# A turned weight block copied in halves, weight casts and x loads moved in the opening, and six units' stores cut in two

## The chip, the core and the metric

The kernel runs on one core of a Trainium2 chip. The metric is the device time of one execution in microseconds (us). The time before is 408.87 us, the median of three runs (406.65 to 410.15).

## The reference

A dynamic convolution over seven taps, whose weights are a softmax per head, feeds a small maxout network:

```python
w = softmax(weight_gen, axis=-1)          # (8, 4160, 8 heads, 7 taps)
x_pad = 6 zero rows ahead of x            # x: (8, 4160, 192)
y[b, s, h, :] = sum_k w[b, s, h, k] * x_pad[b, s + k, h, :]   # 24 features a head
h1, h2 = y @ w1, y @ w2                   # (192, 1024) each
out = maximum(h1, h2) @ w_out             # (1024, 192), float32
```

The setup stretches x to 33280 rows of 192 float32, and the output has the same shape.

## The kernel before

**Tiling.** The 33280 rows are laid over 128 partitions, 260 positions ("columns") each. The columns come in batches: batches 0 to 14 have 16 columns, then one of 12 and one of 8. A batch is cut into units: of 4 columns in batches 0 and 1 (units 0 to 7), of 8 columns afterwards (units 8 to 33), and four more at the end (8, 4, 4, 4). A unit of n columns has n tiles of hidden work; each tile makes 1024 float32 per partition in PSUM, which one relu turns into bf16.

**Arithmetic.** max(h1, h2) is computed as h1 + relu(h2 - h1). So TensorE multiplies the transposed y by wd = w2 - w1 (line 336), ScalarE takes the relu out of PSUM (line 346, "rd_t"), TensorE multiplies that by w_out (line 375), and the linear part y @ (w1 @ w_out) is added by six matmuls with the product w10 (line 387). ScalarE copies the results out (line 431, evac), and SP stores them (line 445).

**Weights.** TensorE contracts 64 rows at a time in pairs, so the 192 rows of wd are kept in six blocks of 512 columns: wd blocks 0, 1 and 2 are differences that VectorE writes (diff, "d.0", "d.1", "d.2", line 593), and blocks 3, 4 and 5 are blocks 0, 1 and 2 with their halves of partitions swapped. TensorE makes the swap (turn, "t.0" to "t.2", line 601), and ScalarE copies it out of PSUM (turn_out, "T", line 607). t.0 and t.2 stand side by side in one PSUM tile, and T.0 copies both at once, into blocks 3 and 5; T.1 copies block 4. The table WD says which blocks a tile reads: those of the first 512 hidden features (tiles 0 and 1 of a 4-column unit, "h.0", "h.1") read blocks 0, 2, 3 and 5, those of the second (h.2, h.3) read blocks 1, 2, 4 and 5. w1 is also cast to bf16 on ScalarE in three parts (cast_w1, "c.0" to "c.2", line 611), is transposed on TensorE ("v", line 628), copied out ("V", line 633), and multiplied by w_out ("p", line 647) to give w10 ("C", lines 654 and 656).

**y.** Softmax weights come from ScalarE and VectorE: exponent ("X", line 153), sum ("n", line 168), log ("l", line 172), subtraction ("s", line 177), exponent again into bf16 pairs ("W", line 191). VectorE multiplies x by them ("m", line 211). In batches 0 and 1 TensorE sums the seven taps and transposes in one go ("y", line 281) and ScalarE copies the result out ("e", line 293). From batch 2 on VectorE adds the taps (lines 227, 233, 236), and a transposing transfer on SP's queue (line 245) brings y into the layout that TensorE reads; a one-element copy on GpSimd ("gate", line 253) waits for its landing, and the next loads of x and weight_gen are issued behind it.

**Order.** The schedule is by hand: each engine runs its instructions in the order in which they are recorded. The opening (batches 0 and 1 up to tile 15) is a string of steps, OPENING; each step is one of the letters above with its arguments. "k.n" are n matmuls on constant data. Loads are "lg" (weight_gen of a batch; batches 0 and 1 on SP's queue, later ones on GpSimd's), "xf" (first x, SP), "lw" and "lt" (the weights, in halves, SP; the arguments are the half and 0 for w1, 1 for w2), "lx" (x, GpSimd's queue, cast to bf16 on the way), "lo" (w_out, GpSimd). "@step" behind a load makes it wait for that step. "xa" and "xv" cast the first x on ScalarE and VectorE. After the opening, a loop over groups of tiles (two or three tiles each, line 780) issues hidden work, results of earlier tiles, and through extra() the VectorE work two units ahead.

**Stores.** evac puts the store of a unit's results on SP's queue when the last columns are copied. Stores of the middle units are held back and issued just behind the next transposing transfer.

Of the kernel before, what the change touches and what calls it, by code (L numbers as in the profile page):

```python
# [23 lines left out]
def kernel(  # L24
# [29 lines left out]
    def dcol(c):  # L54

        return (c + ROT) % CPP
# [207 lines left out]
    def half(j):  # L264
        return slice(64 * j, 64 * j + 64)
# [95 lines left out]

    def op_out(c):

        tile_, at = op_at[c // 2]
        return tile_[:, at + c % 2 * 512:at + c % 2 * 512 + D]

    def out_hidden(c, f, r):

        u, i, j = column(c)
        t0 = TILES.index((u, 0))  # L370
        if UNITS[u][2] == 8:
            (rd, k), at = rd_at[t0 + f], j * 512 + i * P
        else:
            (rd, k), at = rd_at[t0 + f // 2], j * 512 + f % 2 * 256 + i * P
        return nc.tensor.matmul(  # L375
            op_out(c), lhsT=rd[half(r), k * 1024 + at:k * 1024 + at + P],
            rhs=wo[half(r), f * D:(f + 1) * D], start=False, stop=(r != j and f == FCH - 1),
            skip_group_check=True,
        )

# [25 lines left out]
    def relay(last):  # L406

        go = nc.scalar.nop()
        for mm in last:
            tc.add_manual_dep(go.ins, mm.ins.name, SYNC, reason="bank of the other half")  # L410
        return go

    def evac(p, n):

        tile_, at = op_at[p]
        o = o_t[0]
        if p == NT // 2 - 1:

            nc.scalar.copy(out=_sub(o_last, 0, [[D, 2], [1, D]]),
                           in_=_sub(tile_, at, [[512, 2], [1, D]]))  # L420
            for j, eng in enumerate((nc.scalar, nc.sync)):
                eng.dma_start(
                    out=bass.AP(tensor=out.tensor, offset=dcol(place(p)[0] + 2 * j) * D, ap=[[CPP * D, P], [1, D]]),
                    in_=o_last[:, j * D:(j + 1) * D],
                )
            return
        runs = [[q for q in range(p, p + n) if column(2 * q)[0] == u]
                for u in range(column(2 * p)[0], column(2 * (p + n - 1))[0] + 1)]
        for qs in runs:
            c, h = place(qs[0])  # L430
            copied = nc.scalar.copy(out=_sub(o, c % 24 * D, [[D, len(qs)], [h * D, 2], [1, D]]),  # L431
                           in_=_sub(tile_, at + (qs[0] - p) * D, [[D, len(qs)], [512, 2], [1, D]]))
        stores = []
        for q in range(p, p + n):
            u, i, _ = column(2 * q)
            if u == NU - 2 and UNITS[u][2] == 8 and i % 2:
                stores.append((nc.sync, place(q)[0] - 1, [4 * D, 2], [1, 2 * D]))
            elif u < NU - 1 and i == UNITS[u][2] // 2 - 1:
                stores.append((nc.sync, place(q)[0] - i, [1, 2 * (i + 1) * D]))
            if u == NU - 1:  # L440
                stores.append((nc.sync, place(q)[0], [2 * D, 2], [1, D]))
        for eng, c, *ap in stores:

            def issue(eng=eng, c=c, ap=ap, o=o):
                eng.dma_start(
                    out=bass.AP(tensor=out.tensor, offset=dcol(c) * D, ap=[[CPP * D, P], *ap]),
                    in_=_sub(o, c % 24 * D, ap),
                )

            if 3 <= u < NU - 3:  # L450
                held.append(issue)
            else:
                while u > 3 and held:
                    held.pop(0)()
                issue()
        return copied
# [33 lines left out]
    def hidden(g, now=(), between=lambda: None, beside=lambda: None, ahead=lambda: None,  # L490
               before=lambda: None, after=lambda: None):


        t0, n = GROUPS[g]
        rd = room(g)
        for t in range(t0, t0 + n - 1):
            hid_tile(t)
        if now:
            out_room(now, "a" if n == 1 and "a" in ps else None)
            last = out_first(now)  # L500
        for t in range(t0, t0 + n - 1):
            relu(rd, t, 1)
        if now:
            go = relay(last)
        hid_tile(t0 + n - 1)
        before()
        if len(now) > 2:
            beside()
        relu(rd, t0 + n - 1, 1)
        ahead()  # L510
        if now:
            out_second(now, go)
            evac(now[0] // 2, len(now) // 2)
        between()
        after()
        if len(now) <= 2:
            beside()
# [31 lines left out]
    w1 = stage.tile([P, F + HF], BF16, name="w1")  # L549
    w1t = stage.tile([P, FCH * D], BF16, name="w1t")  # L550
# [31 lines left out]
    def block(i):  # L582

        return wd[:, i * HF:(i + 1) * HF]

    def features(i, wi):

        return (ws["T", wi] if i == 2 else ws["E", wi])[:, i % 2 * HF:(i % 2 + 1) * HF]
# [4 lines left out]
        return nc.vector.tensor_tensor(out=block(i), in0=a, in1=b, op=ALU.subtract)  # L593

    turned = {}

    def turn(i):

# [4 lines left out]

    def turn_out(i, v=0):

        n = 2 - i
        return (nc.vector.tensor_copy if v else nc.scalar.copy)(out=_sub(wd, (3 + i) * HF, [[2 * HF, n], [1, HF]]), in_=_sub(turned[i], 0, [[512, n], [1, HF]]))  # L607

    def cast_w1(i):

        return nc.scalar.copy(out=w1[:, i * HF:(i + 1) * HF], in_=features(i, 0))

    def w1_transposed(_):

# [16 lines left out]
    def w1_copy(h):  # L631

        return nc.scalar.copy(out=w1t[:, 4 * h * D:4 * (h + 1) * D], in_=turned["v"][:, h * 1024:h * 1024 + 4 * D])  # L633

    def few(n):

# [13 lines left out]
    def w10_copy(i):  # L650

        pw = turned["w"]
        if i == 0:
            return nc.scalar.copy(out=_sub(w10, 0, [[D, 2], [1, D]]), in_=_sub(pw, 0, [[512, 2], [1, D]]))
        to, frm, at = ((64, 0, 0), (0, 64, 512))[i - 1]
        return nc.scalar.copy(out=w10[to:to + 64, 2 * D:3 * D], in_=pw[frm:frm + 64, at:at + D])

    warm = ps["h"].tile([P, 1024], FP32, name="warm", tag="hd")

# [31 lines left out]
    def results_buffer(_):  # L691
# [28 lines left out]
    """  # L720

    make_identity(nc, ident_f)
# [91 lines left out]
```

## Time and profile before

One execution was profiled. It took 407.24 us, of which 405.4 us are the span from the first to the last instruction; the difference, 1.84 us, lies outside the span.

| what | value |
|---|---|
| runs | 406.65, 408.87, 410.15 us |
| profiled execution | 407.24 us |
| its span | 405.4 us |
| granted TensorE clock | 0.999 of full speed |
| VectorE busy | 369.3 us (91%) |
| ScalarE busy | 361.1 us (89%) |
| GpSimd busy | 69.7 us (17%) |
| HBM traffic | 36.55 MB read, 25.56 MB written |

In the profile's lines, PE is TensorE's matmuls, PEld its weight loads, DVE is VectorE, ACT ScalarE, POOL GpSimd, SP SyncE; "q" behind an engine is its DMA-issuing sequencer. A line such as "L346 ACT ACTIVATE rd_t<-hdp x2" names the kernel's line, the engine, the operation, output and input, and the number of instructions that are merged.

Landings of the opening's transfers, from the semaphores in the trace (us from the span's start):

| step | queue | issued | landed |
|---|---|---|---|
| lg.0 | SP | 0.74 | 4.11 |
| xf, columns -6 to -1 | SP | 1.19 | 5.56 |
| xf, columns 0 to 3 | SP | 1.66 | 7.15 |
| w1, w2 parts (8 transfers, 1.5 MB) | SP | 2.12 to 7.16 | 7.64, 8.22, 8.76, 9.92, 10.46, 11.69, 11.93, 13.20 |
| lg.1 | SP | 7.66 | 15.20 |
| lx.0.4.4 | POOL | 5.96 | 12.73 |
| lx.0.12.4 | POOL | 7.98 | 15.33 |
| lx.0.8.4 | POOL | 12.07 | 16.95 |
| lo | POOL | 12.59 | 19.81 |
| lg.3 | POOL | 13.49 | 20.91 |
| lx.1.0.8 | POOL | 17.15 | 23.41 |

### The profile page before, as it was taken

What the parts mean: (1) busy time and instruction counts of PE and PEld (TensorE: products, weight loads), DVE (VectorE), ACT (ScalarE), POOL (GpSimd) and SP (SyncE); (2) the same over time, 40 slices, a digit from 0 to 9 for tenths busy, and PEclk for the clock granted to TensorE, in tenths of its full rate; (3) what the DMA queues carried; (4) which work ended last, traced back from release to release, by engine and by line L of the source; (5) the groups of instructions that cost most, each with busy time, mean ns of one, the idle gap of its engine ahead of it and who ended that gap; (6) DMA issues with size and microseconds to landing.
All of it is one profiled execution on the core that took longest, in us unless ns stands there. A gap on an engine that the chain in (4) does not pass through costs nothing.

```text
span 405.4 us, 16319 instructions
## 1 busy us (share of the span) xinstructions
PE 396.0 (98%) x7503; PEld 321.1 (79%) x7503; DVE 369.3 (91%) x211; ACT 361.1 (89%) x465; POOL 69.7 (17%) x96
## 2 busy tenths in 40 slices
PE   6999999999999999999999999999999999999996
PEld 2688999777777877777777778777777877787995
DVE  6999999999999999999999999999999999998200
ACT  5999899999999989999899999989999899888872
POOL 2211020212112211122220122121112121210100
PEclk9999999999999999999999999999999999999999
DMA  8955569765877656874776667778457847557304
GB/s 262 247 120 106 155 113 173 188 163 136 164 131 207 175 97 113 251 191 80 213 190 106 146 189 189 91 232 189 78 133 217 170 79 210 136 99 197 100 40 157
DMA packets 60019, 63.16 MB, mean 156 GB/s; under 512 B 47545, under 2 KB 48569, under 8 KB 59952
## 3 DMA queue, kind: packets, MB, share of 16 engines
q1 hardware_dynamic: 51952, 40.15, 37.7%
q0 software_dynamic: 7856, 21.89, 27.4%
q8 instruction: 58, 0.95, 0.9%
q10 hardware_dynamic: 144, 0.10, 0.1%
q14 instruction: 9, 0.07, 0.0%
HBM read 36.55 MB, written 25.56 MB: 153 GB/s over the span
## 4 chain that ended last, share of the span: by engine, by line
PE 94%; DMA 3%; ACT 2%; issue 0%; SPq 0%
PE op_ps L375 42%; PE hdc L336 13%; PE hdb L336 13%; PE hda L336 13%; PE op_ps L387 8%; PE yps L281 2%; PE hdp L336 2%; DMA ws0E<-in_moe_w_dram 1%; DMA xs<-in_x_dram 1%; ACT rd_t L346 1%; PE pw L647 0%; ACT wd L607 0%; ACT e_t L153 0%; ACT w1t L633 0%; ACT yt L293 0%
## 5 line engine op out<-in xcount | busy, mean ns | idle before, releaser
L375 PE MATMUL op_ps<-wo,rd_t 64*128 64x192 bf16 x4160 | 210.6, 243 | 0.6 <-issue 0.6
L375 PEld LDWEIGHTS <-rd_t 64*128 64x128 bf16 x4160 | 180.7, 94 | 15.6 <-issue 0.8
L211 DVE TENSOR_TENSOR m_t<-xb,en_t 128x10752 bf16<-128x10752 bf16 (+2 forms) x39 | 187.5, 4817 | 2.0 <-ACT en_t L191 1.9
L336 PEld LDWEIGHTS <-wd 64*128 64x128 bf16 x1824 | 96.3, 94 | 39.2 <-issue 1.9
L346 ACT ACTIVATE rd_t<-hdc 128x1024 bf16<-128x1024 f32 x82 | 84.0, 1025 | 18.1 <-PE hdc L336 16.5
L253 POOL CAST gate<-yt 128x1 f32<-128x1 bf16 x30 | 37.3, 1243 | 272.3 <-DMA yt<-y_t 272.3
L346 ACT ACTIVATE rd_t<-hdb 128x1024 bf16<-128x1024 f32 x81 | 83.7, 1033 | 0.0
L346 ACT ACTIVATE rd_t<-hda 128x1024 bf16<-128x1024 f32 x81 | 83.4, 1030 | 0.0
L227 DVE TENSOR_TENSOR m_t<-m_t 128x4608 bf16<-128x4608 bf16 (+1 forms) x30 | 72.9, 2431 | 0.1
L336 PE MATMUL hdc<-yt,wd 64*128 64x512 bf16 (+1 forms) x552 | 67.9, 353 | 0.0
L431 ACT COPY o_t<-op_ps 128x384 f32<-128x384 f32 (+1 forms) x99 | 56.0, 577 | 12.6 <-PE op_ps L375 12.6
L336 PE MATMUL hda<-yt,wd 64*128 64x512 bf16 (+1 forms) x540 | 67.0, 355 | 0.0
L336 PE MATMUL hdb<-yt,wd 64*128 64x512 bf16 (+1 forms) x540 | 67.0, 355 | 0.0
L387 PE MATMUL op_ps<-w,yt 64*128 64x192 bf16 x780 | 55.4, 243 | 0.0
L387 PEld LDWEIGHTS <-yt 64*128 64x128 bf16 x780 | 38.8, 94 | 14.6 <-issue 0.3
L233 DVE TENSOR_TENSOR m_t<-m_t 128x3072 bf16<-128x3072 bf16 (+1 forms) x30 | 50.1, 1671 | 0.1
L191 ACT ACTIVATE en_t<-wg_t 128x896 bf16<-128x896 f32 (+3 forms) x48 | 35.4, 769 | 2.3 <-PE op_ps L375 2.0
L236 DVE TENSOR_TENSOR y_t<-m_t 128x1536 bf16<-128x1536 bf16 (+1 forms) x30 | 27.4, 915 | 0.6
L168 DVE TENSOR_REDUCE sum_t<-e_t 128x64 f32<-128x448 f32 (+3 forms) x31 | 19.6, 635 | 3.2 <-ACT e_t L153 3.1
L125 POOL DMA_DIRECT2D xb<-in_x_dram x34 | 18.2, 535 | 24.0 <-ACT en_t L191 12.3
L177 DVE TENSOR_TENSOR wg_t<-wg_t,sum_t 128x280 f32<-128x280 f32 (+6 forms) x46 | 22.0, 480 | 0.0
L153 ACT ACTIVATE e_t<-wg_t 128x896 f32<-128x896 f32 (+2 forms) x18 | 15.8, 884 | 2.1 <-DMA wg_t<-in_weight_gen_dram 2.1
(39 smaller groups left out, 111.3 us busy)
## 6 DMA issues: line engine op xcount, KB each, us to landing
out_dram<-o_t SPq DMA_DIRECT2D x27, 768.0 KB, 4.8
xb<-in_x_dram POOLq DMA_DIRECT2D x30, 384.0 KB, 5.3
wg_t<-in_weight_gen_dram POOLq DMA_DIRECT2D x13, 448.0 KB, 6.0
out_dram<-o_t SPq DMA_DIRECT2D x10, 384.0 KB, 3.3
xb<-xb POOLq DMA_DIRECT2D x7, 288.0 KB, 5.1
wg_t<-in_weight_gen_dram SPq DMA_DIRECT2D x2, 448.0 KB, 5.5
xb<-in_x_dram POOLq DMA_DIRECT2D x4, 192.0 KB, 6.1
xs<-in_x_dram SPq DMA_DIRECT2D x1, 576.0 KB, 4.4
```

The costliest lines, as they stand in the source:

```text
L177: nc.vector.tensor_tensor(out=w_t, in0=w_t, in1=_sub(s_ts[b], hs.start, [[1, hs.stop - hs.start], [0, K]]), op=ALU.subtract)
L191: act = nc.scalar.activation(out=_sub(en_ts[b], (o * WGC + ((i or 0) * J + j) * N * K) * 2, [[2 * N, K], [2, N], [1, 2]]), in_=_sub(wg_ts[ ...
L211: return nc.vector.tensor_tensor(out=m_out, in0=x_in, in1=_sub(en_ts[b], at * H * 2, [[2, K * n * H], [0, G // 2], [1, 2]]), op=ALU.mult,)
L227: nc.vector.tensor_tensor(out=taps(0, 1, 3), in0=taps(0, 1, 3), in1=taps(3, 1, 3), op=ALU.add)
L233: nc.vector.tensor_tensor(out=taps(0, 2, 2), in0=taps(0, 2, 2), in1=taps(1, 5, 2), op=ALU.add)
L236: nc.vector.tensor_tensor(out=_sub(y_ts[b], o * D, [[64, 2], [P, 3 * w // 2], [1, 64]]), in0=taps(0, 1, 1), in1=taps(2, 1, 1), op=ALU.add,)
L253: nc.gpsimd.tensor_copy(out=gate, in_=yt[:, 0:1])
L336: nc.tensor.matmul(hid_out(t, f, j), lhsT=wd_at(j, s, f // 4, f % 4 * P, P), rhs=_sub(yt_ts[u][half(j), :], (s + j) % 3 * P, [[3 * P, w // ...
L346: relu_of[t0] = nc.scalar.activation(out=rd[:, k * 1024:(k + n) * 1024], in_=hd[:, at:at + n * 1024], func=AF.Relu)
L375: return nc.tensor.matmul(op_out(c), lhsT=rd[half(r), k * 1024 + at:k * 1024 + at + P], rhs=wo[half(r), f * D:(f + 1) * D], start=False, s ...
L387: nc.tensor.matmul(op_out(c + j), lhsT=yt_ts[u][half(j), (3 * i + (s + j) % 3) * P:(3 * i + (s + j) % 3 + 1) * P], rhs=w10[half(j), s * D: ...
L431: copied = nc.scalar.copy(out=_sub(o, c % 24 * D, [[D, len(qs)], [h * D, 2], [1, D]]), in_=_sub(tile_, at + (qs[0] - p) * D, [[D, len(qs)] ...
```

## The change

- turn_out learns two more steps: T.3 copies only block 3 and T.4 only block 5, 512 columns each. The opening uses T.3, T.4 and T.1 in place of T.0 and T.1.
- The opening's order is new. On the engines this means the following. SP's loads: the same twelve sizes in the same places, with the third parts of the weights and the second halves of w1 and w2 in other places (the second half of w1 is now ninth instead of eleventh, that of w2 eleventh instead of ninth). VectorE: the cast xv stands between the two subtractions s.0.0 and s.0.1; nothing else moves. ScalarE: xa moves ahead of l.0.1 and W.0.0.0, W.0.12 ahead of c.0 and W.0.8 behind it, c.2 ahead of e.0.0, c.1 ahead of e.0.1; then T.3, T.4, X.1, r.0, T.1, r.1; V.1 comes ahead of V.0; some of the later steps of batches 1 to 3 change places. TensorE: 25 constant matmuls instead of 21 at the start and 3 instead of 11 among the turns; h.0 and h.1 ahead of t.1. GpSimd's queue: lx.0.12.4 waits for W.0.12 instead of xa; lx.0.8.4, lo and lx.1.0.8 no longer wait for a step and follow it directly; lg.2 and lg.3 come behind them.
- Stores of units 19 to 24 (PARTED) are issued as two transfers of 384 KB instead of one of 768 KB.
- out_hidden can take all 128 rows at once, and cast_w1, w1_copy and w10_copy can run on another engine; no call uses that.

```diff
-    def out_hidden(c, f, r):
+    def out_hidden(c, f, r=None):
...
+        rows = slice(0, P) if r is None else half(r)
         return nc.tensor.matmul(
-            op_out(c), lhsT=rd[half(r), k * 1024 + at:k * 1024 + at + P],
-            rhs=wo[half(r), f * D:(f + 1) * D], start=False, stop=(r != j and f == FCH - 1),
+            op_out(c), lhsT=rd[rows, k * 1024 + at:k * 1024 + at + P],
+            rhs=wo[rows, f * D:(f + 1) * D], start=False, stop=(r != j and f == FCH - 1),
...
+    PARTED = range(19, 25)
...
             elif u < NU - 1 and i == UNITS[u][2] // 2 - 1:
-                stores.append((nc.sync, place(q)[0] - i, [1, 2 * (i + 1) * D]))
+                w = i + 1
+                for k in range(0, 2 * w, w if u in PARTED else 2 * w):
+                    stores.append((nc.sync, place(q)[0] - i + k, [1, (w if u in PARTED else 2 * w) * D]))
...
     def turn_out(i, v=0):
 
+        to = (nc.vector.tensor_copy if v else nc.scalar.copy)
+        if i > 2:
+            k = i - 3
+            return to(out=block(3 + 2 * k), in_=turned[0][:, 512 * k:512 * k + HF])
         n = 2 - i
-        return (nc.vector.tensor_copy if v else nc.scalar.copy)(out=_sub(wd, (3 + i) * HF, [[2 * HF, n], [1, HF]]), in_=_sub(turned[i], 0, [[512, n], [1, HF]]))
...
+        return to(out=_sub(wd, (3 + i) * HF, [[2 * HF, n], [1, HF]]), in_=_sub(turned[i], 0, [[512, n], [1, HF]]))
...
     OPENING = """
-        lg.0 xf.-6.6 xf.0.4 lt.1.1 lt.0.0 lw.0.1 lw.0.0 lt.1.0 k.1 lw.1.1 lt.0.1 lw.1.0 lg.1 X.0.0.2 X.0.1.2
-        n.0.0.2 n.0.1.2 l.0.0.2 l.0.1.2 s.0.0.2 k.1 W.0.0.0 s.0.1.2 xa.-6.4 W.0.0.1 W.0.8 xv.-2.6 k.19
-        lx.0.4.4@l.0.0.2 lx.0.12.4@xa.-6.4 m.0.0.0 c.0 W.0.12 m.0.0.1 W.0.4 y.0.0 k.3 y.0.1 e.0.0 c.2 d.0 d.2
-        e.0.1 t.0 k.2 c.1 t.2 k.4 T.0 d.1 t.1 k.2 T.1 m.0.4 lx.0.8.4@W.0.4 lo.0@e.0.0 lg.3@e.0.1 h.0 X.1 r.0
-        h.1 r.1 lx.1.0.8@m.0.4 v.0 n.1 V.0 l.1 h.2 y.1 r.2 e.1 m.0.8 s.1 lg.2@r.2 m.0.12 h.3 r.3 h.4 h.5 V.1
-        r.4 W.1.0 W.1.4 m.1.0 y.2 r.5 e.2 h.6 lx.1.8.8@W.1.0 m.1.4 p.0 C.2 h.7 y.3 C.1 lh.2 C.0 r.6 W.1.8 r.7
-        X.2 n.2 A.3 m.1.8 e.3 B.3 h.8 D.3 r.8 Z.0 E.3 A.4 B.4 lx.2.0.8.0@r.8 h.9 l.2 X.3 W.1.12 y.4 e.4 r.9
-        s.2 D.4 h.10 E.4 W.2.0 n.3 r.10 lg.4@r.10 A.5 y.5 h.11 e.5 l.3 m.1.12 B.5 r.11 D.5 h.12 E.5 A.6 B.6
-        h.13 D.6 r.12 y.6 E.6 W.2.8 lx.2.8.8@W.2.8 r.13 A.7 e.6 h.14 h.15 B.7 r.14 r.15 D.7 y.7 E.7 e.7
+        lg.0 xf.-6.6 xf.0.4 lt.1.0 lt.0.0 k.2 lw.0.1 k.19 lw.0.0 lt.1.1 lw.1.0 lt.0.1 X.0.0.2 k.1 n.0.0.2
+        X.0.1.2 lw.1.1 k.1 k.2 n.0.1.2 l.0.0.2 s.0.0.2 xa.-6.4 l.0.1.2 W.0.0.0 lx.0.4.4@l.0.0.2 lg.1 xv.-2.6
+        W.0.0.1 s.0.1.2 W.0.12 c.0 lx.0.12.4@W.0.12 W.0.8 m.0.0.0 m.0.0.1 W.0.4 y.0.0 y.0.1 c.2 e.0.0 c.1
+        e.0.1 d.0 d.2 t.0 k.3 t.2 T.3 d.1 T.4 h.0 h.1 t.1 X.1 r.0 lx.0.8.4 T.1 lo.0 r.1 m.0.4 n.1 v.0 h.2
+        lx.1.0.8 V.1 y.1 r.2 l.1 h.3 e.1 m.0.8 lg.2@l.1 s.1 V.0 m.0.12 r.3 h.4 W.1.0 m.1.0 y.2 h.5 r.4
+        lg.3@m.0.4 p.0 e.2 r.5 h.6 lx.1.8.8 y.3 W.1.8 h.7 lh.2 C.1 C.0 C.2 A.3 W.1.4 X.2 r.6 e.3 B.3 m.1.4
+        h.8 D.3 y.4 r.7 r.8 Z.0 E.3 n.2 X.3 l.2 m.1.8 A.4 e.4 W.1.12 lx.2.0.8.0@r.7 B.4 h.9 D.4 h.10 r.9 E.4
+        s.2 r.10 lg.4@r.9 y.5 W.2.0 A.5 h.11 B.5 h.12 e.5 D.5 n.3 r.11 r.12 A.6 m.1.12 E.5 h.13 B.6 D.6 y.6
+        r.13 E.6 h.14 e.6 l.3 lx.2.8.8@r.13 h.15 r.14 A.7 W.2.8 B.7 y.7 D.7 r.15 e.7 E.7
```

More of the change, by code (lines that the diff above doesn't have):

```diff
@@ L502, in hidden @@
             relu(rd, t, 1)
-        if now:
-            go = relay(last)
+        go = relay(last) if now else None
         hid_tile(t0 + n - 1)
@@ L595 @@
     turned = {}
+    ENG = (nc.scalar.copy, nc.vector.tensor_copy, nc.gpsimd.tensor_copy)
     def turn(i):
@@ L604, in turn_out, with cast_w1 @@
     def turn_out(i, v=0):
+        to = (nc.vector.tensor_copy if v else nc.scalar.copy)
+        if i > 2:
+            k = i - 3
+            return to(out=block(3 + 2 * k), in_=turned[0][:, 512 * k:512 * k + HF])
         n = 2 - i
-        return (nc.vector.tensor_copy if v else nc.scalar.copy)(out=_sub(wd, (3 + i) * HF, [[2 * HF, n], [1, HF]]), in_=_sub(turned[i], 0, [[512, n], [1, HF]]))
-    def cast_w1(i):
-        return nc.scalar.copy(out=w1[:, i * HF:(i + 1) * HF], in_=features(i, 0))
+        return to(out=_sub(wd, (3 + i) * HF, [[2 * HF, n], [1, HF]]), in_=_sub(turned[i], 0, [[512, n], [1, HF]]))
+    def cast_w1(i, eng=0):
+        if eng == 3:
+            return nc.gpsimd.dma_start(out=w1[:, i * HF:(i + 1) * HF], in_=features(i, 0))
+        return ENG[eng](out=w1[:, i * HF:(i + 1) * HF], in_=features(i, 0))
     def w1_transposed(_):
@@ L629, in w1_products, with w1_copy @@
                                  is_transpose=True, skip_group_check=True)
-    def w1_copy(h):
-        return nc.scalar.copy(out=w1t[:, 4 * h * D:4 * (h + 1) * D], in_=turned["v"][:, h * 1024:h * 1024 + 4 * D])
+    def w1_copy(h, eng=0):
+        return ENG[eng](out=w1t[:, 4 * h * D:4 * (h + 1) * D], in_=turned["v"][:, h * 1024:h * 1024 + 4 * D])
     def few(n):
@@ L648, in w10_product, with w10_copy @@
                                  start=(fi == 0), stop=(fi == FCH - 1), skip_group_check=True)
-    def w10_copy(i):
+    def w10_copy(i, eng=0):
         pw = turned["w"]
         if i == 0:
-            return nc.scalar.copy(out=_sub(w10, 0, [[D, 2], [1, D]]), in_=_sub(pw, 0, [[512, 2], [1, D]]))
+            return ENG[eng](out=_sub(w10, 0, [[D, 2], [1, D]]), in_=_sub(pw, 0, [[512, 2], [1, D]]))
         to, frm, at = ((64, 0, 0), (0, 64, 512))[i - 1]
-        return nc.scalar.copy(out=w10[to:to + 64, 2 * D:3 * D], in_=pw[frm:frm + 64, at:at + D])
+        return ENG[eng](out=w10[to:to + 64, 2 * D:3 * D], in_=pw[frm:frm + 64, at:at + D])
     warm = ps["h"].tile([P, 1024], FP32, name="warm", tag="hd")
```

## The prediction

> **What bounds the kernel now.** I read the page's busy shares and chain first, then busy time by stretches, then the chain of waits of the first 50 us, then the timeline. The page:
>
> ```profile
> span 405.4 us, 16319 instructions
> PE 396.0 (98%) x7503; PEld 321.1 (79%) x7503; DVE 369.3 (91%) x211; ACT 361.1 (89%) x465; POOL 69.7 (17%) x96
> PEclk9999999999999999999999999999999999999999
> ...
> PE 94%; DMA 3%; ACT 2%; issue 0%; SPq 0%
> ```
>
> The clock is granted in full throughout, and TensorE (PE) sets the end; the other 6% of the chain have to lie somewhere early. The stretches (columns: length, then busy us and count of PE, weight loads, DVE, ACT, POOL, then clock, DMA share, GB/s) say where:
>
> ```profile
> 9.70:20.00 10.30, 9.95 (x246) 6.71 (x247) 9.44 (x7) 9.87 (x18) 2.53 (x4) 1.00 1.15 250
> 20.00:30.00 10.00, 9.18 (x284) 8.40 (x285) 10.00 (x5) 9.80 (x18) 1.61 (x3) 1.00 0.55 113
> 30.00:40.00 10.00, 9.35 (x318) 8.90 (x316) 9.89 (x7) 9.89 (x16) 1.07 (x2) 1.00 0.49 112
> 48.60:60.00 11.40, 11.40 (x256) 11.40 (x249) 10.61 (x6) 10.67 (x14) 2.22 (x4) 1.00 0.63 121
> 60.00:370.00 310.00, 310.00 (x5434) 244.91 (x5430) 307.48 (x173) 286.43 (x354) 57.70 (x71) 1.00 0.69 159
> ```
>
> From 48.62 us, where the first matmul of the loop stands (hda), PE never stops. Its work from there is untouched by the change, so the end moves by as much as that matmul moves, unless PE then runs out of input. Before it, PE has holes while VectorE and ScalarE are full. The chain of waits of that stretch (start, us, what) runs over ScalarE:
>
> ```profile
> 7.16 6.03 DMA ws0E<-in_moe_w_dram
> 13.22 0.62 ACT w L611
> 13.84 1.40 ACT wd L607 x2
> 15.24 0.94 ACT e_t L153
> 16.18 1.82 ACT rd_t L346 x2
> ```
>
> The last weight half lands at 13.20; behind it stand, one after another, the cast c.1, both turned copies, the exponent X.1 and the first relus. TensorE waits for all of it.
>
> The one thing that can stop PE later is its input: VectorE makes y, a transfer transposes it, gate shows the landing, hda reads it. Unit 30, the tightest, in the timeline:
>
> ```profile
> 312.42 1.44 SPq L245 DMA_TRANSPOSE yt<-y_t  x1
> ...
> 317.34 0.64 POOL L253 CAST gate<-yt 128x1 f32<-128x1 bf16 x1 [10.16 <-DMA yt<-y_t]
> ...
> 318.99 0.83 PE L336 MATMUL hda<-yt,wd 64*128 64x512 bf16 x6
> ```
>
> It lands 318.99 - 317.34 = 1.65 us before its use. The same difference is 13.97 us for unit 8, 8.5 for unit 15, 5.0 for unit 22, 2.1 for unit 32 and 2.4 for unit 34, since VectorE needs some 11.84 us per unit (from one y_t to the next) and PE 11.45. VectorE is never idle for more than 0.8 us between 13.3 and 364 us, so it can't follow if PE moves ahead.
>
> **The change part by part.** I walked both orders along the engines: each instruction starts when its engine is free and what it reads is there, with durations from the timeline. Pitch is a duration less about 0.1 us of overlap, as neighbouring rows show. On the order of before the walk puts the first hda at 48.21 (trace 48.62; it leaves out fetch holes of PE, 0.65 us at 39.27 for one). So I use it for differences only.
>
> *VectorE.* xv waits for its data until 7.24 and ends at 8.00; s.0.1 (0.62, pitch 0.53) now stands behind it instead of in the hole ahead of it. The first product m.0.0.0 therefore starts at about 8.48 instead of 8.11: a cost of 0.37 us. d.0 starts at 11.41 instead of 11.05, d.2 ends at 12.7 as before (its data land at 11.93), and d.1 waits for the eleventh load, 13.20, as before. There the delay ends: m.0.4 stays at 13.90, and all of VectorE behind it stays. This cover is 0.5 us thick; without it all of VectorE would be late by the remainder.
>
> *Casts and halves on ScalarE.* The second half of w1 now lands in the ninth place (11.69 in before), so c.1 runs at about 12.45 instead of 13.22, ahead of e.0.1 (13.44 at its end). T.3 and T.4 cost 0.47 pitch each (row of 512 columns: 0.59), against 0.90 + 0.58 for T.0 and T.1, and T.1 moves behind r.0. So three copies cost 1.42 instead of 1.48, nothing. T.4 ends at 14.57, and ScalarE is free for X.1 at 14.44 instead of 15.22: 0.78 us sooner. h.0 reads blocks 0, 2, 3 and 5, which need d.0 and d.2 alone; on PE h.0 and h.1 finish by 16.05 instead of 16.28.
>
> *X.1 and lg.1.* X.1 needs lg.1, which lands at 15.20 in before, just when X.1 wants it. Now it is wanted at 14.44, with r.0, T.1 and every later relu queued behind it on ScalarE. This is the number that decides. In before lx.0.12.4 (issued 7.98) shared the DMA engines with lg.1 (7.66): by the trace's packet records GpSimd's queue took 31 of the 48 us of engine time (16 engines) from 12.0 to 15.0, the last third of them for lx.0.8.4. Now lx.0.12.4 waits for W.0.12 and is issued at about 9.3, with lx.0.8.4 (9.8), lo (10.3) and lx.1.0.8 (11.2) behind it. lx.0.4.4's first packet came 3.4 us after its issue had ended (6.67 to 10.0). With the same lag lx.0.12.4 starts at 13.1 instead of 12, and lg.1 has the engines for an additional microsecond or so. If it got the half it shared, 1.0 us, it would land at 14.2; if nothing changes, at 15.2. I take the middle, 14.7. The walk gives hda at 47.30, 47.46 and 47.96 for 14.2, 14.7 and 15.2, so 0.91, 0.75 or 0.25 us sooner than its 48.21.
>
> *x sooner.* VectorE's m.0.8 (17.76), m.1.0 (24.50) and m.1.8 (31.43) have their x at 16.95, 23.41 and 28.36 in before, so sooner loads take no wait away. lg.2 and lg.3 now follow l.1 (19.7): landing near 25, wanted at 27.1 and 32. Zero, covered by 2 us.
>
> *Matmuls on constants* stand where PE waits anyway; 25 end at 9.6, and y.0.0 starts at 10.1. Zero.
>
> *Stores in two.* Six more issues on SP, some 0.38 us each, all behind the transposing transfers of units 23, 24, 26 and 27; SP then waits 8 us or more for VectorE (217.9 us of waits for y_t in total). The landing of a transposition beside them may move; those four have 5.4, 5.1, 4.2 and 2.8 us to spare, 2.0 the thinnest after PE's advance. Zero; if that cover goes, each further 1 us is lost once. A transfer of 768 KB lands 4.8 us after its issue and one of 384 KB after 3.3 (page, medians), so the first half may even land sooner.
>
> **Sum.** 0.75 us off, at 405.4 + 1.84 = 407.24 of the profiled execution: 406.5. That execution is the second lowest of the four times there are; their median is 408.05, and the runs alone give 408.87. Four times of which none is disturbed spread over 3.5 us, four times the step in question. I put the new time at 408.05 - 0.7 = 407.4.
>
> **Rivals.** 1. *lg.1 doesn't come sooner*: the two queues share the engines as long as both have packets, and lx.0.12.4 is in the queue before lx.0.4.4 has ended (12.2). For it: from 12.5 to 14.0 the queues' busy times were about equal (13.2 and 12.8 us). Against: at 7 to 10 us GpSimd's queue got nothing although lx.0.4.4 had been issued. Then 0.25 us is left: 407.8. The Trainium skill, "DMA: Bandwidth & Descriptors", Queues, rings and completion order, says that each engine goes round between the queues it has work for, packet by packet, which is this rival; the equal shares agree, the silence from 7 to 10 us does not.
>
> 2. *Slower: lg.1 comes later, and ScalarE stands at X.1.* lx.0.8.4, lo and lx.1.0.8 are in the queue 2 to 6 us sooner than in before, and from 10.5 to 11.5 GpSimd's queue held nearly all the engines (SP's moved 60 of 210 KB). If that recurs at 13, lg.1 waits for lx.0.12.4 and lx.0.8.4. It decides at 15.45: from there each microsecond of lg.1 is one of the end. lx.0.8.4 took 1.62 us behind lx.0.12.4, so lg.1 at up to 16.8, 1.35 us slower than before: 409.4. With lo (2.86 us) in front too, 4.2: 412.3.
>
> 3. *PE runs out of y.* The 0.75 us come off every lead, so unit 30 has 0.9 left. Its landing took 4.92 us from the issue, others 3.9 to 5.4. If one comes 1 us late, PE waits a little, and part of the gain goes back: 407.8 to 408.
>
> 4. *The turned halves don't free h.0*: ruled out, since in the built order T.1 stands behind r.0 and h.0's reads of blocks 3 and 5 wait for T.3 and T.4 only.
>
> **Numbers.** Forecast 0.50 (0.5 to 0.9 us off), rival 1 0.22, rival 2 0.13, rival 3 0.10, others 0.05. A measurement of this kernel tells about 1%, 4.1 us, from no change. No case but the last end of rival 2 reaches that, so within 1% gets 0.88; the spread of the runs alone (406.65 to 410.15) leaves 0.06 on either side. The range: the runs' own spread less 0.7 is 405.9 to 409.5; rival 2 takes the upper end to 410.0, and sooner lg.1 and chance in the median the lower end to 405.3. The forecast's own range is 405.9 to 409.0.
>
> **What would show it.** In the new profile: c.1 (L622) near 12.5; T.3 and T.4 (L614) at 13.5 and 14.0; X.1 (third L153) at 14.4 to 14.8, with lg.1's landing as releaser if later than 14.45; m.0.4 at 13.9 and unit 8's last y_t still ending at 51.05; the first hda at 47.9 (48.62 - 0.75); unit 30's lead 0.9; the span 404.7. It is wrong if hda stands above 48.6 or if PE waits anywhere between hda and the end.

## The result and the profile after

The changed kernel takes 406.43 us (median of 22 runs, 405.89 to 409.46), the kernel before, run beside it, 408.92 us (22 runs, 406.65 to 412.15). The ratio is 0.9945 (95% interval 0.9929 to 0.9961): about half a per cent faster, and the times lie closer together. Measured beside each other twice more, the two kernels stood at 406.45 against 408.13 and at 406.42 against 408.76.

The profiled execution of the changed kernel took 407.22 us, which is one of its slower ones, and that of before 407.24, one of the faster ones of its kernel; so these two pages show equal spans, and the gain can't be read from them. The page after:

```profile
span 405.4 us, 16322 instructions
PE 395.5 (98%) x7499; PEld 321.8 (79%) x7499; DVE 369.2 (91%) x211; ACT 361.0 (89%) x466; POOL 68.2 (17%) x96
...
PEclk9999999999999999999999999999999999999999
...
PE 94%; ACT 3%; DMA 2%; SPq 1%; issue 1%
```

What they do show is where things stand. The stretches (columns as before):

```profile
20.00:30.00 10.00, 7.33 (x246) 6.79 (x247) 9.83 (x5) 9.94 (x18) 2.17 (x4) 1.00 0.51 134
30.00:40.00 10.00, 10.00 (x342) 10.00 (x338) 9.13 (x6) 8.67 (x14) 1.07 (x2) 1.00 0.56 133
40.00:48.60 8.60, 8.60 (x306) 8.60 (x304) 8.53 (x4) 7.67 (x11) 0.53 (x1) 1.00 0.49 124
48.60:60.00 11.40, 11.40 (x246) 11.40 (x243) 11.40 (x8) 10.89 (x15) 2.57 (x4) 1.00 0.55 113
60.00:370.00 310.00, 310.00 (x5437) 245.57 (x5434) 307.56 (x173) 286.52 (x354) 55.90 (x71) 1.00 0.68 159
```

PE is now full from 30 us on, where before it had holes until 45, and has a large hole between 20 and 30 us instead. The timeline of PE names it:

```profile
25.44 1.33 PE L281 MATMUL yps<-around,m_t 64*128 64x64 bf16 x80
28.74 0.23 PE L281 MATMUL yps<-around,m_t 64*128 64x64 bf16 x4 [1.96 <-issue]
28.79 0.83 PE L336 MATMUL hdp<-yt,wd 64*128 64x256 bf16 x12
```

After 80 of the 84 matmuls of y.3, PE waits 1.96 us for nothing that the profile shows ("issue"). The records of the DMA queues show what for: a transfer of 16 KB on a queue of kind "instruction" starts at 26.30 us and ends at 27.20. That queue moves 58 such transfers in the execution, 0.95 MB for PE's 14,998 instructions, 63 bytes each: it carries PE's program (the last section counts this out). From here on such a gap is called a program hole.

ScalarE's timeline, the changed place of the opening:

```profile
12.88 0.63 ACT L622 CAST w<-ws0E 128x512 bf16<-128x512 f32 x1
...
13.79 1.07 ACT L614 CAST wd<-turned 128x512 bf16<-128x512 f32 x2
14.80 0.95 ACT L153 ACTIVATE e_t<-wg_t 128x896 f32<-128x896 f32 x1
15.67 1.02 ACT L346 ACTIVATE rd_t<-hdp 128x1024 bf16<-128x1024 f32 x1
16.64 0.58 ACT L616 CAST wd<-turned 128x512 bf16<-128x512 f32 x1
```

That is c.1, T.3 and T.4 (one row), X.1, r.0 and T.1 in the order that the change gives them. X.1 starts 0.02 us behind the landing of lg.1 (14.78). And unit 30, whose input is the tightest, in the timeline:

```profile
318.13 0.29 POOL L253 CAST gate<-yt 128x1 f32<-128x1 bf16 x1 [10.51 <-DMA yt<-y_t]
319.36 0.83 PE L336 MATMUL hda<-yt,wd 64*128 64x512 bf16 x6
```

It lands 1.23 us before its use (1.65 before), so PE didn't have to wait for it.

### The profile page after: what moved, and what is told of

It reads as the page before. It is cut to its first block, busy times and chain, and to the rows that moved or that the text cites. A ratio compares the mean times of both kernels' runs of the same rounds, so it can differ in the third digit from the quotient of the medians.

```text
span 405.4 us, 16322 instructions
## 1 busy us (share of the span) xinstructions
PE 395.5 (98%) x7499; PEld 321.8 (79%) x7499; DVE 369.2 (91%) x211; ACT 361.0 (89%) x466; POOL 68.2 (17%) x96
## 4 chain that ended last, share of the span: by engine, by line
PE 94%; ACT 3%; DMA 2%; SPq 1%; issue 1%
PE op_ps L376 42%; PE hdc L336 13%; PE hda L336 13%; PE hdb L336 13%; PE op_ps L388 8%; PE hdp L336 2%; PE yps L281 2%; DMA ws0E<-in_moe_w_dram 2%; ACT rd_t L346 1%; ACT yt L293 0%; PE pw L658 0%; ACT en_t L191 0%; SPq L574 0%; ACT w L622 0%; ACT wd L614 0%
## 5 line engine op out<-in xcount | busy, mean ns | idle before, releaser
L376 PEld LDWEIGHTS <-rd_t 64*128 64x128 bf16 x4160 | 181.0, 94 | 14.7
L346 ACT ACTIVATE rd_t<-hdc 128x1024 bf16<-128x1024 f32 x82 | 84.0, 1025 | 17.9 <-PE hdc L336 16.1
L346 ACT ACTIVATE rd_t<-hda 128x1024 bf16<-128x1024 f32 x81 | 83.4, 1030 | 0.2 <-ACT o_t L434 0.2
L346 ACT ACTIVATE rd_t<-hdb 128x1024 bf16<-128x1024 f32 x81 | 83.6, 1032 | 0.0
L253 POOL CAST gate<-yt 128x1 f32<-128x1 bf16 x30 | 35.7, 1189 | 274.8 <-DMA yt<-y_t 274.8
L388 PEld LDWEIGHTS <-yt 64*128 64x128 bf16 x780 | 39.1, 94 | 14.5 <-issue 0.3
L346 ACT ACTIVATE rd_t<-hdp 128x1024 bf16<-128x1024 f32 x16 | 16.4, 1039 | 1.7 <-PE op_ps L376 1.3
```

The lines of the kernel that those rows point to most:

```text
L253: nc.gpsimd.tensor_copy(out=gate, in_=yt[:, 0:1])
L346: relu_of[t0] = nc.scalar.activation(out=rd[:, k * 1024:(k + n) * 1024], in_=hd[:, at:at + n * 1024], func=AF.Relu)
L376: return nc.tensor.matmul(op_out(c), lhsT=rd[rows, k * 1024 + at:k * 1024 + at + P], rhs=wo[rows, f * D:(f + 1) * D], start=False, stop=(r ...
L388: nc.tensor.matmul(op_out(c + j), lhsT=yt_ts[u][half(j), (3 * i + (s + j) % 3) * P:(3 * i + (s + j) % 3 + 1) * P], rhs=w10[half(j), s * D: ...
```

## The experiments

There are twelve more runs. From their traces, and the two above, come the same few numbers, in us ("last matmul to end" counts from the start of that matmul):

| profiled run | lg.1 landed | X.1 starts | first hda | program holes before it | hda less X.1 less holes | last matmul to end |
|---|---|---|---|---|---|---|
| before | 15.20 | 15.22 | 48.62 | 0.80 | 32.60 | 4.15 |
| e3_before (the same) | 17.55 | 17.57 | 51.73 | 1.92 | 32.24 | 4.16 |
| after | 14.78 | 14.80 | 48.99 | 1.94 | 32.25 | 3.79 |
| e4_after (the same) | 14.87 | 14.89 | 48.17 | 1.11 | 32.17 | 3.80 |
| g3_after_again (the same) | 13.95 | 14.26 | 47.65 | 1.07 | 32.32 | 3.79 |
| e1_whole | 15.27 | 15.29 | 49.43 | 1.54 | 32.60 | 4.15 |
| e2_parted | 15.47 | 15.72 | 49.61 | 1.35 | 32.54 | 3.79 |
| f1_lx_early | 17.44 | 17.46 | 51.39 | 0.88 | 33.05 | 3.81 |
| f2_before_lx_late | 16.09 | 17.30 | 50.57 | 1.03 | 32.24 | 4.16 |
| f3_no_halves | 14.57 | 14.59 | 48.46 | 1.71 | 32.16 | 3.79 |
| f4_lg3_sooner | 14.24 | 14.48 | 47.36 | 0 | 32.88 | 3.79 |
| g4_lg3_again | 14.26 | 14.58 | 47.63 | 0 | 33.05 | 3.80 |
| g2_lg3_v1 | 14.93 | 14.95 | 47.99 | 0.27 | 32.77 | 4.00 |
| g1_x_as_before | 14.93 | 16.68 | 49.37 | 0.40 | 32.29 | 3.79 |

"Program holes" are the gaps from one matmul's start to the next's of over 0.33 us between 25 us and the first hda, each less the 0.22 us that a full matmul takes. Two entries of that column are something else: the 0.27 of g2_lg3_v1 and the 0.40 of g1_x_as_before are waits for a relu of ScalarE ("<-ACT rd_t L346"). And program holes ahead of 25 us stand in the next column instead: by the same measure 0.41 us in f4_lg3_sooner, 0.58 in g4_lg3_again and 0.32 in g2_lg3_v1, all at 22 us, and 0.15 at 23 us in before. From the first hda to the start of the last matmul it is 352.66 us in thirteen of the fourteen, and 354.01 in e2_parted, which has one more program hole there (1.44 us from start to start, at 65.8 us). So an execution's span is X.1's start, the holes, the rest up to hda, 352.66 and the tail, added up (for before 15.22 + 0.80 + 32.60 + 352.66 + 4.15 = 405.43).

**The stores, taken out and alone.** e1_whole is the changed kernel with no unit's store in two; e2_parted is the kernel before with the stores of units 19 to 24 in two.

```diff
-    PARTED = range(19, 25)
+    PARTED = range(0)
```

```diff
-                stores.append((nc.sync, place(q)[0] - i, [1, 2 * (i + 1) * D]))
+                w = i + 1
+                for k in range(0, 2 * w, w if 19 <= u < 25 else 2 * w):
+                    stores.append((nc.sync, place(q)[0] - i + k, [1, (w if 19 <= u < 25 else 2 * w) * D]))
```

> The changed kernel with every middle unit's store whole again (768 KB); the opening stays new. Theory A (the whole step is won in the opening, 48 us): as the changed kernel, ratio 0.994 to 0.996 to the kernel before. Theory B (the two-part stores carry most of it): ratio 0.998 to 1.000, with single times up to 409 to 412 us as the kernel before has them, and a wait of about 2 us somewhere between 200 and 300 us in a profile that catches it. A share in between would say that both carry some: forecast of the opening alone, 0.75 us, is a ratio of 0.998.

> The kernel before with one thing changed: stores of units 19 to 24 in two transfers. Theory A (opening): ratio 1.000, times spread from 406.7 to 412 us as before. Theory B (stores): ratio 0.996 or lower, a median near 407 us, and the spread gone.

Measured: e1_whole 407.05 us (406.27 to 408.06, 12 runs; ratio to before 0.9974, 0.9958 to 0.9990); e2_parted 407.50 (406.31 to 409.72, 12 runs; 0.9995, 0.9974 to 1.0015), with half of its runs below 406.9 and half above 408.1. The ratio of e1_whole lies between the two theories, that of e2_parted fits Theory A, and a third of a microsecond is within the noise of both; the traces tell more. Neither trace has a hole of PE between 190 us and the end, and neither do those of before and after: at the place of the divided stores nothing changes. But the last column of the table does: 4.15 without the divided stores, 3.79 with them, whatever the rest of the kernel. The last two stores land at the same distance behind the start of the last matmul in all (2.6 us for SP's, 2.8 for ScalarE's). What differs is what SP does then. At the end it goes through a list of waits, one or two semaphores each, 0.061 us apart (a semaphore here is the counter by which a transfer tells that it has landed). Transfers take the semaphores of their queue kind in turn, so six more transfers move the last store from the third wait of the list (it lands at 404.88 us in e1_whole, and seven more waits follow) to the last but one of ten (403.63 in e4_after, with one to follow). The stores in two parts are worth 0.36 us, at the very end, by their number alone.

**Each kernel once more.** e3_before and e4_after are the two kernels unchanged.

> The kernel before, unchanged, for a second profile and a measure of noise: ratio 1.000 within 0.2%, median near 408.9 us. Its profiled execution was among the fastest of its 22 times (407.24 against a median of 408.92 us); a second one nearer the median should show where the usual 1.7 us more are lost. Theory A: in the first 50 us (first hda later than 49 us). Theory B: after 190 us, with the first hda at 48.6 us.

> The changed kernel, unchanged, for a second profile: ratio 0.9945 within 0.2%. Its profiled execution was among its slower ones (407.22 against a median of 406.43 us) and shows 2.0 us in which TensorE waited for nothing that the profile names (26.7 to 28.7 us). If that is a chance event, a profile at 406.4 us has none, and its first hda stands about 0.8 us sooner, near 48.2 us; the forecast was 47.9.

Measured: e3_before 408.35 us (406.91 to 410.96, 12 runs; ratio to the shared runs of before 1.0008, 0.9988 to 1.0029); e4_after 406.45 (406.40 to 411.09, 7 runs; 0.9974, 0.9942 to 1.0007, an interval that the one run at 411.09 us widens beyond 1). The hole of PE at 26 us is no chance event: the profiled execution of e4_after, at 406.41 us, has it too (1.33 us from start to start), and its first hda stands at 48.17. The profiled execution of e3_before took 410.33 us, so it shows what the first profile of before didn't; its first hda at 51.73 us is Theory A's case. The chain of waits in it:

```profile
8.05 9.49 DMA wg_t<-in_weight_gen_dram
17.55 0.02 issue
17.57 0.95 ACT e_t L153
18.52 1.82 ACT rd_t L346 x2
```

lg.1 took 9.49 us to land, 7.54 in the first profile of before (7.66 to 15.20), and 6.52 to 7.13 in the three of the changed kernel. Its issue varies as well: in all fourteen traces SP issues lg.1 within 0.05 us of the landing of the fourth load of its queue (lands at 7.64, issued at 7.66 in before; 8.04 and 8.05 here; 7.42 and 7.43 in g3_after_again). ScalarE stands still for 1.14 us for it, with all relus behind. And PE's timeline has two large program holes:

```profile
42.21 0.34 PE L375 MATMUL op_ps<-wo,rd_t 64*128 64x192 bf16 x4 [0.94 <-issue]
...
47.31 0.50 PE L281 MATMUL yps<-around,m_t 64*128 64x64 bf16 x22 [0.98 <-issue]
```

The first profile of before has them at the same places of the program, at 39 and 44 us, of 0.89 and 0.34 us from start to start. The changed kernel has none there, and one of 1.29 to 2.15 us at 26 us. A late lg.1 is not all that makes before slow: e2_parted, which has its opening, took 409.19 us in its profiled execution with lg.1 at 15.47 and three program holes of 0.89, 0.89 and 1.44 us.

**GpSimd's loads sooner still.** f1_lx_early is the changed kernel with lx.0.12.4 behind xa.

```diff
-lx.0.12.4@W.0.12
+lx.0.12.4@xa.-6.4
```

> The changed kernel, but lx.0.12.4 waits for xa again, which ends at 6.5 us here: lx.0.12.4, lx.0.8.4, lo and lx.1.0.8 are all issued some 2.7 us sooner (7.0 to 9.0 instead of 9.7 to 11.7). Theory 1, the landing of lg.1 against GpSimd's loads sets the end (in the five profiles so far the first hda stands 32.2 to 32.8 us behind that landing, holes of TensorE for its program not counted): lg.1 shares the engines with more of GpSimd's packets, lands at 16 to 18 instead of 14.8, and the end comes 1 to 3 us later: 407.5 to 409.5. Rival, SP's own queue sets that landing: lg.1 at 14.8 give or take 0.4, 406.2 to 406.9.

Measured: 408.53 us (407.65 to 409.63, 12 runs; ratio to before 1.0004, 0.9982 to 1.0026), 2.1 us above the changed kernel's median beside other runs of before (406.42 to 406.45). The profiled execution is the slowest of the twelve (409.63 us). ScalarE's timeline:

```profile
13.48 1.07 ACT L614 CAST wd<-turned 128x512 bf16<-128x512 f32 x2
17.46 0.95 ACT L153 ACTIVATE e_t<-wg_t 128x896 f32<-128x896 f32 x1 [2.91 <-DMA wg_t<-in_weight_gen_dram]
```

ScalarE waits 2.91 us for lg.1, which lands at 17.44 although it was issued at 7.46, sooner than in all other traces but one. From 12 to 15 us GpSimd's queue took 27.3 us of engine time and SP's 25.8; in the first profile of the changed kernel SP's queue took 15.6 of 16.8 us from 12 to 13, and lg.1 was all but through by 14. The span of f1_lx_early's profile is 3.23 us longer than that of e4_after: X.1 comes 2.57 us later, and the stretch from there to hda is 0.88 us longer, with TensorE at half its rate from 20.1 to 23.5 us (last section). Theory 1 holds for loads that come sooner: lg.1 lands later and the end moves with it. The Trainium skill, "DMA: Bandwidth & Descriptors", Queues, rings and completion order, has each engine go round the queues that have packets; the near-equal shares of f1_lx_early agree with that.

**That load's wait alone.** f2_before_lx_late is the kernel before with W.0.12 ahead of c.0 and lx.0.12.4 behind it.

```diff
-lx.0.12.4@xa.-6.4 m.0.0.0 c.0 W.0.12
+W.0.12 lx.0.12.4@W.0.12 m.0.0.0 c.0
```

> The kernel before with one part of the change alone: W.0.12 ahead of c.0, and lx.0.12.4 waiting for it, so issued near 9.7 instead of 8.0; lx.0.8.4 and what follows keep their waits. Theory 1: lg.1 lands at 14.7 to 15.3 in every execution instead of 15.2 to 17.5, so the median falls by 1.0 to 1.7 us, to 406.5 to 407.2, and the times lie closer together. Rival, the order on TensorE and ScalarE makes the gain: it falls by less than 0.5 us.

Measured: 407.87 us (406.93 to 409.18, 12 runs; 1.0001, 0.9984 to 1.0019), beside 408.24 for before. Theory 1 expected at least 1.0 us; the medians differ by 0.37, and the interval holds zero and ends at 0.65. This part alone doesn't carry the change. Its profiled execution is the slowest of the twelve (409.18 us). In it lg.1 took 7.03 us from issue to landing, as in the changed kernel, but it was issued only at 9.06, behind a fourth load that landed at 9.04, and TensorE ran at half its rate from 12.2 to 15.6 us, so that X.1 started 1.21 us behind lg.1. What holds the other eleven runs it doesn't show.

**No halves.** f3_no_halves is the changed kernel with T.0 for T.3 and T.4.

```diff
-t.2 T.3 d.1 T.4 h.0 h.1 t.1 X.1
+t.2 T.0 d.1 h.0 h.1 t.1 X.1
```

> The changed kernel with T.0, which copies blocks 3 and 5 in one instruction, in the place of T.3 and T.4. Theory 1: T.0 takes 0.90 where T.3 and T.4 take 0.96 together, so X.1 starts at the landing of lg.1 (14.8) as before, the first relu follows it, and nothing changes: 406.2 to 406.8, first hda within 0.3 us once the hole at 26.6 us is taken off. Rival, the halves carry the gain, since h.0 starts 0.5 us later without them: 406.9 to 407.4.

Measured: 406.69 us (406.14 to 409.46, 12 runs; 0.9973, 0.9954 to 0.9992), 0.26 above the changed kernel's median beside other runs of before; X.1 0.02 us behind lg.1, as in two of the three traces of the changed kernel, and the rest up to hda 32.16 us, as in the changed kernel (32.17 to 32.32). Copying the block in halves is worth nothing that can be seen; two of the twelve runs, at a mean clock of 0.996, took 408.74 and 409.46 us and widen the interval, so some tenths of a microsecond aren't ruled out. The order of T.1 and X.1, which both have, is another matter, and no run tests it.

**One load out of the burst.** In the changed kernel GpSimd issues lg.2, lg.3 and lx.1.8.8 from 20.3 to 21.9 us, 1.28 MB together, and the DMA engines are all but full from 22 to 26 us (21 to 25 in g3_after_again); PE's program transfer starts at 24.92 to 26.30 us in its three traces. f4_lg3_sooner lets lg.3 go behind lx.1.0.8.

```diff
-lx.1.0.8 V.1 y.1
+lx.1.0.8 lg.3 V.1 y.1
...
-lg.3@m.0.4 p.0
+p.0
```

> The changed kernel with lg.3 right behind lx.1.0.8 and with no wait, so issued at 12.2 instead of 20.8: 448 KB leave the 1.28 MB of loads that GpSimd issues at 20.3 to 21.9, and fall into 19.5 to 21 us, where the queues moved next to nothing. Theory 2, TensorE's hole at 26.6 us (1.3 and 2.15 us from start to start in two profiles of the changed kernel) is its program's transfer of 16 KB standing behind that burst: the transfer ends about 1 us sooner, the hole falls below 0.8 us, and the time to 405.2 to 405.9. Rival, the hole belongs to that place in the program whatever the queues carry: hole as before, 406.2 to 406.6.

> The changed kernel as it is, beside the others on the same chip: 406.1 to 406.7, lg.1 at 14.5 to 15.3, a hole of 1 to 2.2 us at 26 to 27 us and none of over 0.4 us between 30 us and the first hda, a tail of 3.79 us.

> The run f4_lg3_sooner again, beside the changed kernel on the same chip. Theory 2: no hole above 0.5 us at 26 us, 405.5 to 406.1, and faster than the changed kernel of the same call by 0.4 us or more. Rival, its lower time was chance: within 0.2 us of the changed kernel.

Measured: f4_lg3_sooner 405.99 us (405.06 to 407.94, 12 runs; ratio to before 0.9957, 0.9940 to 0.9975), just above the 405.2 to 405.9 expected; again, 405.74 (405.42 to 406.87, 6 runs; 0.9937, 0.9917 to 0.9957), beside the changed kernel's 406.42 (405.92 to 407.45, 7 runs; 0.9947, 0.9927 to 0.9967). In g3_after_again lg.1 landed at 13.95, sooner than the 14.5 expected; its hole (1.29 us) and its tail (3.79) came as expected. PE in f4_lg3_sooner:

```profile
21.10 1.29 PE L281 MATMUL yps<-around,m_t 64*128 64x64 bf16 x76
22.82 0.29 PE L281 MATMUL yps<-around,m_t 64*128 64x64 bf16 x8 [0.44 <-issue]
...
25.80 1.54 PE L281 MATMUL yps<-around,m_t 64*128 64x64 bf16 x84
27.16 0.83 PE L336 MATMUL hdp<-yt,wd 64*128 64x256 bf16 x12
```

The hole in y.3 is gone: its program transfer ran from 24.62 to 25.51 us, ahead of its use. The transfer before it, 19.2 to 19.4 in the three traces of the changed kernel, starts at 20.47, among the packets of lg.3 (landed 22.07), which the edit put there, and a smaller hole of 0.44 us opens in y.2. So the traffic decides which transfer is late; the rival, a hole at its place whatever the queues carry, falls. f4_lg3_sooner has the lowest times of the study, its medians 0.4 and 0.7 us under the changed kernel's (the first against other runs of before); the intervals of the two overlap, so the size of that isn't settled.

**x as before.** g1_x_as_before is the changed kernel with the waits of the kernel before on lx.0.8.4, lo, lg.3, lx.1.0.8 and lx.1.8.8.

```diff
-X.1 r.0 lx.0.8.4 T.1 lo.0 r.1 m.0.4
+X.1 r.0 lx.0.8.4@W.0.4 T.1 lo.0@e.0.0 lg.3@e.0.1 r.1 m.0.4
...
-lx.1.0.8 V.1
+lx.1.0.8@m.0.4 V.1
...
-lg.3@m.0.4 p.0 e.2 r.5 h.6 lx.1.8.8 y.3
+p.0 e.2 r.5 h.6 lx.1.8.8@W.1.0 y.3
```

> The changed kernel with one part undone: lx.0.8.4, lo, lg.3, lx.1.0.8 and lx.1.8.8 wait for the steps they waited for in the kernel before (lx.0.12.4 keeps W.0.12). Theory 2, TensorE's hole at 26.6 us comes of the burst that these loads make from 20.3 us: lg.3 is issued near 13, lx.1.8.8 near 23, the hole falls below 0.5 us, and the time to 405.3 to 406.0, so the sooner loads cost time. Rival, sooner loads are part of the gain: products of VectorE wait for x, or lg.1 lands later beside lg.3, 406.8 to 408.

Measured: 407.82 us (407.34 to 408.98, 12 runs; 0.9981, 0.9966 to 0.9997). The hole at 26 us is gone, as Theory 2 expected, and no program hole is left ahead of hda; yet it is 1.4 us slower than the changed kernel beside it. That is the rival's number without the rival's reasons: in its profiled execution no product of VectorE waits for x, and lg.1 lands at 14.93. There X.1 stands 1.75 us behind the landing of lg.1, mostly since TensorE ran at half its rate and the turned block came late (last section). But only three of its twelve runs show a lower mean clock, and the other nine stand at 407.34 us or above too. What holds those isn't seen.

**One copy later, and one more store in two.** g2_lg3_v1 is f4_lg3_sooner with V.1 behind e.1 and PARTED = range(19, 26).

```diff
-lx.1.0.8 lg.3 V.1 y.1 r.2 l.1 h.3 e.1 m.0.8
+lx.1.0.8 lg.3 y.1 r.2 l.1 h.3 e.1 V.1 m.0.8
```

> The changed kernel with lg.3 right behind lx.1.0.8 as in the run f4_lg3_sooner, the copy V.1 behind e.1 instead of ahead of r.2, and the store of unit 25 in two transfers too (seven units instead of six). In f4_lg3_sooner the chain of waits runs over ScalarE until 20.45 us and from there over TensorE without a wait of 0.5 us, so taking V.1 (0.69 us) out of it should bring the first hda 0.4 to 0.7 us sooner: 46.7 to 47.0, if no new hole opens; unit 30 then keeps some 0.4 us of lead. Theory 3, the closing waits: with one more transfer the last store lands on the ninth semaphore of SP's list of waits instead of the eighth, so the span ends 3.73 us behind TensorE's last matmul (3.79 in all profiles with six units in two, 4.15 in all with none). The time: 405.1 to 405.7. Rival: tail as with six units, and time as f4_lg3_sooner, 405.8 to 406.2.

Measured: 406.16 us (405.70 to 407.99, 9 runs; 0.9941, 0.9924 to 0.9958); the first hda 33.04 us behind X.1, as in f4_lg3_sooner (32.88) and g4_lg3_again (33.05). The hda and the tail came otherwise than expected, and the time is the rival's. The chain of waits now stays on ScalarE until 29.8 us: V.1 was moved along a full engine, not off it. And the tail is 4.00, not 3.73: with seven more transfers ACT's store takes the last wait of the list, but SP's, which lands 0.17 us sooner, takes the third, and the seven waits behind that (0.49 us to the last one's end) end later than ACT's store. What counts is the later of landing plus waits behind it, over both stores.

## Why the prediction was right, and where it was off

The forecast of 407.4 us, within 1% of before, held with 406.43. That tests little: any step of up to 4.1 us would have stayed within 1%. The prediction expected 0.5 to 0.9 us, or one of three worse cases, and the step was 1.7 to 2.5; it came within 1.0 us of the time in part by luck, as its start of 408.05 lay 0.87 below the median of before, 408.92. By its own steps:

**PE from the first hda on.** Right: 352.66 us from hda to the last matmul in both kernels, and no wait of PE in between (e2_parted has one, of 1.44 us). The end moved as hda moved, less what the tail gives.

**VectorE.** Nearly right: m.0.0.0 at 8.70 instead of the 8.48 foreseen, m.0.4 at 14.04 instead of 13.90 (14.11 and 13.49 in the other two traces). Unit 8's last y_t ended at 52.38, 51.56 and 51.05, where 51.05 was said. Part of the lateness is m.0.4's own; in the first profile VectorE also waits for ScalarE, 0.17 us at 27.6 and 0.87 at 34.6. Whether the program hole makes these waits isn't shown.

**ScalarE.** Right within 0.4 us: c.1 at 12.41 to 12.88, where 12.45 was said, T.3 at 13.31 to 13.79, where 13.5 was said, and X.1 at 14.26 to 14.58 where lg.1 was there before it (g3_after_again, f4_lg3_sooner, g4_lg3_again); 14.44 was foreseen.

**lg.1.** Right in two of three: 14.78, 14.87 and 13.95 us in three executions of the changed kernel, 14.7 taken, 14.2 to 15.2 as the ends. (The lag that the estimate used is 3.55 us in the trace, 6.66 to 10.21, not 3.4.) It still decides: in two of the three X.1 starts 0.02 us behind it.

**The size.** This is the step that was mis-sized. "0.78 us sooner" was counted from X.1 at 15.22 us, where lg.1 had landed in the one profiled execution of before. In another it landed at 17.55. The mean of the two traces of before against the three of the changed kernel gives, from the table: X.1 16.40 to 14.65, that is -1.75; program holes 1.36 to 1.37, nothing; the rest up to hda 32.42 to 32.25, -0.17; the tail -0.36. The mean spans differ by 2.26 us, and the medians of the three comparisons by 2.49, 1.68 and 2.34. The two traces of before stand on either side of its median, but the split rests on five executions; with e2_parted and e1_whole, which share the two openings, X.1 goes from 16.17 to 14.81, that is -1.36. So X.1 is the largest part, 1.4 to 1.75 us where 0.78 was counted. The prediction had put itself on the median, 408.05 less 0.7, but took from it only what the fast execution could lose; that part of the spread is the wait that the change shortens wasn't seen. Why lg.1 lands sooner is only in part shown: GpSimd's loads sooner make it late (f1_lx_early), but holding lx.0.12.4 back in the kernel before gained nothing clear (f2_before_lx_late).

**x sooner: zero.** Wrong in its reason. VectorE has no wait for x to lose, as said; what the loads do to others was costed for lg.1 alone. Their place matters on both sides: 2.7 us sooner costs 2.1 us (f1_lx_early), back to the old waits costs 1.4 (g1_x_as_before, cause open), and the burst that follows from them costs PE a program hole of 1.3 to 2.15 us from start to start at 26 us. In the sum the change pays nothing for that hole, since the old ones, at 39 and 44 us, went.

**Matmuls on constants: zero.** Not tested by itself. In the profile after they lasted until y.0.0 at 10.53 us, where 9.6 and 10.1 had been said, because TensorE came to full rate later (7.65 us instead of 5.56); in e4_after, with full rate from 5.29 us, they ended at 9.43.

**Stores in two: zero.** Right about SP and the landings (unit 30 keeps 1.23, 1.19 and 1.59 us of lead in the three traces; 0.9 was foreseen; the landings that it gives as 3.9 to 5.4 us span 3.2 to 6.2 in the trace). It missed the 0.36 us at the end, which the profile of before could have shown: the last store lands 2.8 us behind the last matmul, and the span ends 1.4 us later still.

**The rivals.** Rival 1 needed lg.1 at 15.2 or later; the changed kernel's three traces don't have it, but e1_whole, with the same opening, has it at 15.27. Rival 2 is real, and f1_lx_early is its case: lg.1 at 17.44, the median 2.1 us higher. In the change itself lx.0.12.4 was held back far enough (9.8 instead of 8.0 us). Rival 3 didn't come. "Wrong if hda above 48.6" struck the profile after (48.99) and not the other two (48.17, 47.65): by the program hole, which the condition didn't allow for.

## What to carry to other kernels

One profiled execution is one draw: where the runs of a kernel spread more than the step at stake, look for the waits that spread (here one landing of 6.5 to 10 us, and the program holes) and cost the change against their usual value, not against the one in the page. Gaps of TensorE that end at "issue" can be its program coming late; before loads are brought forward, see what they pile up behind and which program transfer comes then. Look behind the last store as well: the closing list of waits is part of the time.

## What the hardware showed

**PE's program comes by DMA and can be late.** A hole ends 1.3 to 1.6 us after the end of a 16 KB transfer on the instruction queue: in e3_before transfers ended at 40.72 and 45.96 us and PE went on at 42.21 and 47.31; in the three traces of the changed kernel they ended at 27.20, 26.39 and 25.82, and PE went on at 28.74, 27.91 and 27.40. The places where a hole can stand are fixed: counting PE's matmuls and weight loads from the first, it stops after 961 of them in the changed kernel, after 1729 and 1985 in before, after 705 in f4_lg3_sooner and after 3009 in e2_parted, all multiples of 256 apart, and the transfer that ends just before it goes on is the third, the sixth, the seventh, the second and the eleventh, one for each 256. In all fourteen traces no such block of 256 starts less than 1.27 us behind the end of its transfer. What differs is when the transfer starts: in the changed kernel the third starts 2.9 to 3.9 us after PE passed count 705, while the queues are full, and the fifth to seventh 0.5 to 0.8 us after PE passed the count 256 ahead of theirs. The Trainium skill, "Runtime: NRT & Kernel Launch", Instruction fetch mechanics, has programs refilled in blocks of 16 KiB while the current one runs, at a cost mostly hidden. The block size agrees (16,384 bytes a transfer), and so does the hiding at most blocks; at those above, beside full queues, it was not hidden.

**TensorE fell back to half rate within a short lull.** In g1_x_as_before (columns as before; the granted clock is the third value from the end):

```profile
8.70:12.16 3.46, 1.52 (x47) 0.80 (x46) 3.46 (x4) 2.60 (x8) 0.54 (x1) 0.99 1.10 266
12.16:15.60 3.44, 3.44 (x47) 1.73 (x47) 3.02 (x4) 1.80 (x4) 1.99 (x3) 0.51 1.04 264
15.60:19.00 3.40, 2.73 (x39) 1.80 (x40) 3.00 (x3) 3.27 (x5) 0.53 (x1) 1.00 1.30 222
```

After 3.46 us in which PE was busy for 1.52, with waits of 1.25 and 0.68 us, the granted clock is 0.51 for the next 3.44 us, and a matmul that turns a block takes 0.61 instead of 0.38 us. In e4_after PE was busy for 2.01 of the same 3.46 us, and nothing fell. The same happens in f2_before_lx_late after a wait of 2.34 us (PE busy for 1.23 of 3.41 us) and in f1_lx_early after one of 2.39 us (0.83 of 3.41), each time for 3.41 us. Busy time alone doesn't set the limit: at the end of g2_lg3_v1 PE was busy for 1.49 us from 399.4 to 402.8, and the clock stayed until 406.2. The Trainium skill, "TensorE: Matmul & The Clock Gate", Part 1, has the clock fall after an idle window of some 3.4 us; the length of the slow stretch agrees, but none of these waits was that long. The mean clock of a run hints at it: of the 36 runs of the changed kernel, the two at 0.996 and 0.994 took 409.46 and 411.09 us.
